# Linear attention before a mixture of experts: float32 projections in row halves, numerators in column halves, denominators in column quarters

## The chip, the cores and the metric

The kernel runs on one core of a Trainium2 chip. The metric is the device time of one execution in microseconds. Three timed runs of the kernel before gave a median of 1389.53 us (1389.01 to 1392.44).

## What is computed

Attention with feature maps, for 4 batches and 8 heads of 576 tokens with 64 features; then two layers of feed-forward networks on the 2304 tokens. The change is in the attention alone.

```python
def phi(x):
    proj = np.einsum('bhsd,df->bhsf', x, w_phi)                 # 64 -> 128 features
    proj = proj - np.max(np.abs(proj), axis=-1, keepdims=True)
    return np.concatenate([np.exp(proj), np.exp(-proj)], axis=-1)
q_p, k_p = phi(q), phi(k)
kv = np.einsum('bhsf,bhsd->bhfd', k_p, v)
z = np.sum(k_p, axis=2)
num = np.einsum('bhsf,bhfd->bhsd', q_p, kv)
den = np.einsum('bhsf,bhf->bhs', q_p, z)[..., None] + 1e-06
x = num / den       # then x = moe(x), and out = moe2(x)
```

## The kernel before

**Stages.** The attention stage treats 16 pairs of heads (4 batches by 4 pairs). The first 24 groups of products of the first MoE layer (12 up, 12 down, for the first 1536 tokens) are woven into it. The rest of that layer, and the second layer, come after it and are not edited. Up products for a block of 512 tokens need the attention outputs of every pair whose batch lies in that block, so the first block needs pairs 0 to 3.

**The order** of the attention stage is made ahead, in Python, by the class Plan. Each operation has a name, costs for the engines that may run it, the operations that it follows, a rank, and the buffers that it takes and reads. Plan.run takes again and again the operation that can begin first by these costs, ties by the lower rank (table RANK plus the pair's number). What it takes is emitted, and each engine then runs its instructions in that order.

**One pair of heads, by operations.**

- ld: DMAs on SP's queue bring k and q (128 rows: 64 features of each of two heads; 576 columns) and v. The ring kr, qr has one buffer each.
- two: k and q are split into a rounded high part (kh, qh, a cast on ScalarE or VectorE) and the rest (kl, ql, a subtraction on VectorE or GpSimd, L325).
- P (project, L339): for each of five token tiles (four of 128, one of 64) three float32r products over 256 columns, L348 to L350, against the block-diagonal weights wbh and wbl. Tiles go in units of two, two and one, each in one PSUM bank.
- R and S (largest L355, less L362): VectorE takes the largest magnitude of each row and subtracts it, into pmk and pmq.
- E: two exponentials of keys into ke (L368).
- KV (key_values, L379): v by ke, plain float32, one head in each column half of the array, so two products at a time. The sums over tokens (L387, ones by ke) go to the other half of the same PSUM bank, in column quarters. From pair 5 on (NZ) the four whole tiles are first added in pairs (Z, L392) and summed by add_up (L396).
- CV, TV, VH: key-values and sums are copied out (kvs), turned by TensorE (L409, and L411 for the sums) and copied into kvt, where each head's 128 columns hold 64 of key-values and 64 times the sums.
- T (turn_queries, L430) and X (L437): the queries are turned, ten transposes a pair, and the two exponentials taken into qe.
- A (attend, L447): per head and per half of the tokens (256 and 320) two plain float32 products with 128 weight columns, so that numerators and denominators come in one bank.
- D, N (take): denominators and numerators are copied out, four copies each, 64 rows high, into den and num (L144 is the copy helper).
- I (invert, L459 to L462): VectorE transposes the denominators in 32 by 32 blocks, adds 1e-6, takes the reciprocal, and transposes back.
- X0, X1, X2 (x_part): multiply, round, subtract, giving Xh and Xl for the MoE layer.

**Buffers.** PSUM has five banks in ring "bank" for P, T, TV and A, one bank "kv" for key-values and sums, and two banks "mm" for the woven MoE products (tile names mm; the same lines L231 and L252 serve the later ones as up and dn). Pair p may start its projections in the plan once the last A of pair p - 2 is placed (AHEAD = 2).

**Weights.** The first MoE layer's weights arrive as 64-bit words and are decoded in steps W, L554 to L565, by ScalarE, VectorE and GpSimd, in the same stage (tile acc_a).

Of the kernel before, what the change touches and what calls it, by code (L numbers as in the profile page):

```python
# [33 lines left out]
TILES = [(t * P, min(P, S - t * P)) for t in range(-(-S // P))]  # L34
UNITS = [(0, 1), (2, 3), (4,)]
HALVES = [(0, 256), (256, 320)]
HMAX = 320
# [14 lines left out]
    ld=6.41, sp=11.67, Pk=-7.81, Pq=-3.81, E=11.17, Z=-20.34, KV=-7.89, TV=-14.97, Q=-17.39, A=-0.59, F=2.88,  # L52
    W=22.69, U=16.42, G=5.73,
# [6 lines left out]
class Plan:  # L60
# [6 lines left out]
    WINDOW = 4096 / 1.2  # L67

    def __init__(self):
        self.ops, self.bufs, self.readers, self.begun = {}, {}, {}, set()  # L70

    def op(self, name, costs, after, rank, emit, alloc=(), reads=(), behind=(), late=0):
        self.ops[name] = (costs, after, rank, emit, alloc, {*after, *behind}, late)
        for x in reads:
            self.readers.setdefault(x, []).append(name)

    def run(self):
# [10 lines left out]
        def room(name):  # L88
            t = ready[name]
            for ring, key in self.ops[name][4]:  # L90
                if len(taken[ring]) >= self.bufs[ring]:
                    for x in self.readers[ring, taken[ring][-self.bufs[ring]]]:
                        t = max(t, done.get(x, np.inf))
            return t

        while ready:
            found = []
            for name in ready:
                t = room(name)
                if t < np.inf:  # L100
                    costs, rank = self.ops[name][0], self.ops[name][2]
                    begin = lambda e: max(t, free.get(e, self.START))
                    e = min(costs, key=lambda e: begin(e) + costs[e] + BIAS.get(e, 0))
                    found.append((begin(e), rank, order[name], name, e))
# [3 lines left out]
            cost = costs[e]  # L108
            if e == "t":
                k = int(start // self.WINDOW)  # L110
# [28 lines left out]
def fused(ctx: ExitStack, tc: tile.TileContext, qT, kT, v_main, v_tail, w_phi, alpha, probs, w64, wup, wdn, out):  # L139
# [19 lines left out]
    wbh = const.tile([P, 2, F], F32R, name="wbh")  # L159
    wbl = const.tile([P, 2, F], F32R, name="wbl")  # L160
# [4 lines left out]

    w0 = acc[0][:, 0, :2 * F].rearrange("p (h f) -> p h f", h=2)
# [110 lines left out]
    with ExitStack() as st1:  # L277
# [8 lines left out]
        for args in (  # L286
            ("kr", 1, F32, P, S), ("qr", 1, F32, P, S), ("v", 1, F32, P, len(TILES), 2, D),
            ("kh", 1, F32R, P, S), ("kl", 1, F32R, P, S), ("qh", 1, F32R, P, S), ("ql", 1, F32R, P, S),
            ("m", 13, F32, P, 4), ("pmk", 2, F32, P, 4, F), ("pmq", 3, F32, P, 4, F), ("ke", 2, F32, P, 4, 2, F),
            ("kvs", 1, F32, P, 4, F), ("qe", 4, F32, P, 2, HMAX), ("kvt", 4, F32, P, 4, P),  # L290
            ("den", 2, F32, P, S), ("dt", 1, F32, P, S), ("num", 2, F32, P, S), ("di", 3, F32, P, S // 32, 1),
            ("zsum", 1, F32, P, 4, 2 * F), ("gh", 4, F32R, P, BLK), ("gl", 4, F32R, P, BLK), ("t", 2, F32, P, BLK),
        ):
            ring(*args)
# [3 lines left out]
        ones = pool("ones", 1, st1).tile([P, 32], F32, name="ones")  # L298
# [21 lines left out]
        def two(name, key, src, srckey, n, after, prio, view=lambda x: x, shape=lambda x: x):  # L320

            op((name, "h", *key), hi_cost(n), after, prio, alloc=[(name + "h", key)],
               emit=lambda e: cp(engines[e], shape(new(name + "h", key)), view(tl[src, srckey])))
            op((name, "l", *key), lo_cost(n), [(name, "h", *key)], prio, alloc=[(name + "l", key)], reads=[(src, srckey)],
               emit=lambda e: engines[e].tensor_tensor(  # L325
                   shape(new(name + "l", key)), view(tl[src, srckey]), f32(shape(tl[name + "h", key])), ALU.subtract))

        pairs = [(b, j) for b in range(B) for j in range(NP)]

        def load(p, n):  # L330
            b, j = pairs[p]
            if n == "v":
                v = new("v", p)
                nc.sync.dma_start(v[:, :4], v_main[b, j])
                nc.sync.dma_start(v[:D, 4], v_tail[b, j])
            else:
                nc.sync.dma_start(new(n + "r", p), (qT if n == "q" else kT)[b, j])

        def project(p, n, u):  # L339
            xh, xl = tl[n + "h", (p,)], tl[n + "l", (p,)]  # L340
            unit = UNITS[u]
            rows = TILES[unit[0]][1]
            ps = new("bank", (n, p, u)).rearrange("p (m f) -> p m f", f=F)
            new("pm" + n, (p, u))
            for i, tile_ in enumerate(unit):
                o = ps[:rows, 2 * i:2 * i + 2, :]
                tok = slice(TILES[tile_][0], TILES[tile_][0] + rows)
# [4 lines left out]
        def largest(p, n, u):  # L352
            m, rows = 2 * len(UNITS[u]), TILES[UNITS[u][0]][1]
            ps = tl["bank", (n, p, u)].rearrange("p (m f) -> p m f", f=F)
            nc.vector.tensor_reduce(  # L355
                new("m", (n, p, u))[:rows, :m], ps[:rows, :m], AX.X, ALU.max, apply_absolute_value=True)

        def less(p, n, u):
            m, rows = 2 * len(UNITS[u]), TILES[UNITS[u][0]][1]
            ps = tl["bank", (n, p, u)].rearrange("p (m f) -> p m f", f=F)  # L360
            mx = tl["m", (n, p, u)][:rows, :m, None].to_broadcast([rows, m, F])
            nc.vector.tensor_tensor(tl["pm" + n, (p, u)][:rows, :m], ps[:rows, :m], mx, ALU.subtract)  # L362

        def exp_keys(p, u):
            m, rows = 2 * len(UNITS[u]), TILES[UNITS[u][0]][1]
            e = new("ke", (p, u))
            for s, sc in ((0, 1.0), (1, -1.0)):
                nc.scalar.activation(e[:rows, :m, s], tl["pmk", (p, u)][:rows, :m], AF.Exp, scale=sc)  # L368

        flat = lambda x: x.rearrange("p i s f -> p i (s f)")  # L370

        def key_values(p, u):

            unit = UNITS[u]
            rows, e, v = TILES[unit[0]][1], flat(tl["ke", (p, u)]), tl["v", p]
            kv = new("kv", p) if u == 0 else tl["kv", p]
            for i, tile_ in enumerate(unit):
                for h in range(2):
                    nc.tensor.matmul(  # L379
                        kv[h * D:(h + 1) * D, 0], v[:rows, tile_, h], e[:rows, 2 * i + h],  # L380
                        start=tile_ == 0, stop=tile_ == len(TILES) - 1, skip_group_check=True)
            if p >= NZ and u < 2:
                return
            for i, tile_ in enumerate(unit):
                for h in range(2):
                    r = 32 * (2 * (tile_ % 2) + h)
                    nc.tensor.matmul(  # L387
                        kv[r:r + 32, 1], ones[:rows], e[:rows, 2 * i + h],
                        start=False, stop=tile_ + 2 >= len(TILES), tile_position=(0, r), skip_group_check=True)

        def sum_keys(p, e):
            engines[e].tensor_tensor(new("zsum", p), flat(tl["ke", (p, 0)]), flat(tl["ke", (p, 1)]), ALU.add)  # L392

        def add_up(p):
            for m in range(4):
                nc.tensor.matmul(tl["kv", p][32 * m:32 * m + 32, 1], ones, tl["zsum", p][:, m],  # L396
                                 start=False, stop=True, tile_position=(0, 32 * m), skip_group_check=True)
# [15 lines left out]
        def copy_kv(p, k, e):  # L413
            b = tl["bank", ("kv", p)]
            o = tl["kvt", p].rearrange("p (h s) d -> p h s d", h=2)
            if k == 0:
                cp(engines[e], o[:, :, :, :D], b[:, :2 * P].rearrange("p (s h d) -> p h s d", s=2, h=2))
            else:
                z = b[:, 2 * P:3 * P].rearrange("p (s h d) -> p h s d", s=2, h=2)[:, :, :, 0:1]
                cp(engines[e], o[:, :, :, D:], z.to_broadcast([P, 2, 2, D]))  # L420

        def turn_queries(p, h, c):
            c0, n = HALVES[c]
            ps = new("bank", ("t", p, h, c))
            new("qe", (p, h, c))
            for u, unit in enumerate(UNITS):
                for i, tile_ in enumerate(unit):
                    t0, rows = TILES[tile_]
                    if c0 <= t0 < c0 + n:
                        nc.tensor.transpose(  # L430
# [532 lines left out]
```

## Time and profile before

| what | before |
|---|---|
| median of three runs | 1389.53 us |
| span of the profiled execution | 1389.4 us |
| TensorE busy | 1375.0 us, 99% |
| weight loads busy | 1166.5 us, 84% |
| VectorE busy | 779.9 us, 56% |
| ScalarE busy | 510.4 us, 37% |
| GpSimd busy | 283.1 us, 20% |

Busy times of TensorE include the time in which a product passes through the array while the next has begun, so a busy share of 99% is not a peak. The chain of waits is better to read: it follows back, from the last instruction, what released each step, and gives each piece the time by which it moved the chain on. A plain float32 product stands in the trace as two passes, each with a weight load (PEld); a float32r product and a transpose as one.

### The profile page before, as it was taken

Reading aid. Unit: us, or ns where it says so; the run is one execution under the profiler, and the core shown is the slowest. Engines: PE = TensorE matmul, PEld = TensorE weight load, DVE = VectorE, ACT = ScalarE, POOL = GpSimd, SP = SyncE. Lnnn points to the kernel's source line nnn. Section 1 sums busy time; section 2 is a strip of 40 time slices with the busy share of each in tenths; the row PEclk is TensorE's granted clock in tenths of the full one; section 3 lists DMA queues with packets and bytes.
Section 4 is the critical chain, followed back from the end, with each engine's and each line's share of the span. In section 5 each row is a group of like instructions: output and inputs, shape, how many; then the busy total and the mean of one; then the engine's idle time right before and its main releaser. Section 6 shows DMA issues by size and latency. Waiting matters only on the chain.

```text
span 1389.4 us, 19497 instructions
## 1 busy us (share of the span) xinstructions
PE 1375.0 (99%) x7216; PEld 1166.5 (84%) x7216; DVE 779.9 (56%) x1298; ACT 510.4 (37%) x1115; POOL 283.1 (20%) x278
## 2 busy tenths in 40 slices
PE   8999999999999999999999999999999999999998
PEld 5667767778888888889899889998999899989997
DVE  7995655679958855476445544633334363433342
ACT  6886666643213112125344443321222132211220
POOL 2344334222103004016556651000000000000000
PEclk9999999999999999999999999999999999999999
DMA  4322111022301103007977776665566667655541
GB/s 142 99 80 52 52 51 52 11 78 94 102 0 46 46 0 121 1 16 240 324 247 258 252 260 219 210 219 167 167 190 195 191 207 226 195 174 167 181 153 46
DMA packets 102207, 192.24 MB, mean 138 GB/s; under 512 B 11616, under 2 KB 12768, under 8 KB 102112
## 3 DMA queue, kind: packets, MB, share of 16 engines
q1 hardware_dynamic: 102112, 191.00, 42.7%
q8 instruction: 57, 0.93, 0.3%
q14 instruction: 38, 0.31, 0.1%
HBM read 140.10 MB, written 50.86 MB: 137 GB/s over the span
## 4 chain that ended last, share of the span: by engine, by line
PE 94%; DMA 2%; DVE 2%; ACT 1%; issue 0%; SPq 0%; POOL 0%; POOLq 0%; DVEq 0%; ACTq 0%
PE dn L871 28%; PE up L824 24%; PE up L231 12%; PE dn L252 12%; PE bank L447 4%; PE kv L379 3%; PE mm L252 2%; PE bank L348 2%; PE mm L231 2%; PE bank L430 2%; PE bank L349 1%; PE bank L350 1%; PE kv L387 1%; DMA w<-wdn 1%; PE kv L396 0%; DMA acc_a<-w 0%
## 5 line engine op out<-in xcount | busy, mean ns | idle before, releaser
L871 PE MATMUL dn<-whd,Xh 128*128 128x512 f32 x720 | 231.6, 391 | 0.0
L882 DVE SCALAR_TENSOR_TENSOR acc<-dn,pr,acc 128x512 f32<-128x512 f32 x126 | 88.7, 749 | 190.9 <-PE dn L871 190.9
L824 PE MATMUL up<-Xl,wlu 128*128 128x384 f32 x864 | 158.8, 335 | 1.3 <-DVE c L837 0.9
L871 PEld LDWEIGHTS dn<-whd,Xh 128*128 128x128 f32 x720 | 135.3, 188 | 26.9
L824 PEld LDWEIGHTS up<-Xl,wlu 128*128 128x128 f32 x864 | 150.3, 188 | 2.7 <-DVE c L837 1.8
L871 PE MATMUL dn<-Xh 128*128 128x512 f32 x648 | 151.8, 390 | 0.0
L837 DVE TENSOR_TENSOR c<-up,p 128x384 f32<-128x384 f32 x96 | 53.5, 557 | 175.1 <-PE up L824 175.1
L842 ACT COPY p<-up 128x384 f32<-128x384 f32 x48 | 23.0, 480 | 326.7 <-PE up L824 326.7
L871 PEld LDWEIGHTS dn<-Xh 128*128 128x128 f32 x648 | 121.7, 188 | 25.4
L871 PE MATMUL dn<-wld,Xh 128*128 128x512 f32 x360 | 141.0, 392 | 0.0
L824 PE MATMUL up<-Xl,whu 128*128 128x384 f32 x576 | 111.8, 335 | 0.8 <-ACT p L842 0.8
L831 ACT ACTIVATE Xh<-c 128x384 fp32r<-128x384 f32 x144 | 75.6, 526 | 79.7 <-DVE c L837 79.7
L824 PEld LDWEIGHTS up<-Xl,whu 128*128 128x128 f32 x576 | 101.2, 188 | 1.1 <-ACT p L842 1.1
L231 PE MATMUL up<-Xl,whu 128*128 128x512 f32 (+1 forms) x272 | 99.2, 365 | 0.0
L252 PE MATMUL dn<-gh,wld 128*128 128x512 f32 (+1 forms) x272 | 99.2, 365 | 0.0
L231 PE MATMUL up<-Xh,whu 128*128 128x512 f32 (+1 forms) x272 | 99.2, 365 | 0.0
L252 PE MATMUL dn<-gh,whd 128*128 128x512 f32 (+1 forms) x272 | 99.2, 365 | 0.0
L231 PE MATMUL up<-Xh,wlu 128*128 128x512 f32 (+1 forms) x272 | 99.2, 365 | 0.0
L252 PE MATMUL dn<-gl,whd 128*128 128x512 f32 (+1 forms) x272 | 99.2, 365 | 0.0
L176 ACT CAST gh<-t 128x512 fp32r<-128x512 f32 (+1 forms) x68 | 38.6, 569 | 149.3 <-DVE t L243 149.3
L832 DVE SCALAR_TENSOR_TENSOR Xh<-c,Xh 128x384 fp32r<-128x384 f32 x144 | 85.4, 594 | 5.5
L871 PEld LDWEIGHTS dn<-wld,Xh 128*128 128x128 f32 x360 | 67.6, 188 | 12.9
(171 smaller groups left out, 2498.7 us busy)
## 6 DMA issues: line engine op xcount, KB each, us to landing
whu<-wsu SPq DMA_DIRECT2D x96, 256.0 KB, 3.5
wlu<-wsu SPq DMA_DIRECT2D x96, 256.0 KB, 3.4
st<-w SPq DMA_DIRECT2D x24, 512.0 KB, 3.6
wsu<-whu SPq DMA_DIRECT2D x48, 256.0 KB, 3.3
wsu<-wlu SPq DMA_DIRECT2D x48, 256.0 KB, 3.2
Xh<-wsd SPq DMA_DIRECT2D x48, 256.0 KB, 3.8
wld<-wsd SPq DMA_DIRECT2D x40, 256.0 KB, 3.1
whd<-wsd SPq DMA_DIRECT2D x40, 256.0 KB, 3.4
```

Of the source, the lines that this page charges most:

```text
L176: nc.scalar.copy(hi, src)
L231: nc.tensor.matmul(ps[:, :bn], a[:, cs], x[:, cc, t0:t0 + bn], start=n == 0, stop=n == 3 * CC - 1)
L252: nc.tensor.matmul(ps, w[:, sl], g, start=start and k == 0, stop=stop and k == 2)
L348: nc.tensor.matmul(o, xh[:, tok], wbh, start=True, stop=False)
L379: nc.tensor.matmul(kv[h * D:(h + 1) * D, 0], v[:rows, tile_, h], e[:rows, 2 * i + h], start=tile_ == 0, stop=tile_ == len(TILES) - 1, skip ...
L447: nc.tensor.matmul(nd[:, :n], tl["kvt", p][:, 2 * h + s], tl["qe", (p, h, c)][:, s, :n], start=s == 0, stop=s == 1)
L824: nc.tensor.matmul(ps[name], w[k][:, r, kt * P:(kt + 1) * P], slots[k][:, x + kt], start=start and n == 0, stop=stop and n == 5, skip_grou ...
L831: nc.scalar.activation(gh, src, AF.Relu)
L832: nc.vector.scalar_tensor_tensor(gl, src, 0.0, f32(gh), ALU.max, ALU.subtract)
L837: nc.vector.tensor_tensor(o, ps[name], x, ALU.add)
L871: nc.tensor.matmul(ps[m], x[:, sl], w, start=c == chunks[0] and k == 0, stop=c == chunks[-1] and k == 2)
L882: nc.vector.scalar_tensor_tensor(av, ps[m], pe, av, ALU.mult, ALU.add)
```

## The change

- Projections are plain float32 products of the unsplit k and q with w_phi. Each head uses one half of the array's rows (64 features), the two heads write to two PSUM banks, and each bank takes four token tiles of 128 columns. The splits (two) and the tiles kh, kl, qh, ql, wbh, wbl go.
- The last 64 tokens of k and q of both heads go into one bank, with a head in each half of the columns (project_tails), so that a tile of tails has all 128 rows. R and S follow banks: four of 512 columns and one of 256 for a pair.
- Key-values: as before in column halves, in two parts instead of three; the tail's product takes all 128 rows against a v tile with zeros in the other head's rows (vts, two tiles zeroed once). The sums come after them in one operation (add_up), the tails with ones that are zero in the other head's rows.
- Queries are turned in nine transposes, not ten; the exponentials take 512 columns.
- Numerators: both heads at once, a head in each column half, 288 tokens a product. Denominators: an operation of their own, AD, in four groups of 32 columns (head by half of the tokens). VH becomes one copy.
- invert reads the denominators from PSUM; the reciprocals go, in eight instructions on 32 partitions and nine columns, to the rows in which the second transpose wants them. num is multiplied by the new tile rb.
- Z is two operations, one for each head. Rings: kr and qr have two buffers, pmq, ke, qe, kvt and others change, as the diff shows.
- Plan gets a mode for each TensorE operation (row, col, quarter, full, rounded), adds 100 ns to its cost at a change of mode and 0.57 to its rank there; RANK has other values (W from 22.69 to 40.35 among them).

Its core:

```diff
-            ("kr", 1, F32, P, S), ("qr", 1, F32, P, S), ("v", 1, F32, P, len(TILES), 2, D),
-            ("kh", 1, F32R, P, S), ("kl", 1, F32R, P, S), ("qh", 1, F32R, P, S), ("ql", 1, F32R, P, S),
-            ("m", 13, F32, P, 4), ("pmk", 2, F32, P, 4, F), ("pmq", 3, F32, P, 4, F), ("ke", 2, F32, P, 4, 2, F),
-            ("kvs", 1, F32, P, 4, F), ("qe", 4, F32, P, 2, HMAX), ("kvt", 4, F32, P, 4, P),
-            ("den", 2, F32, P, S), ("dt", 1, F32, P, S), ("num", 2, F32, P, S), ("di", 3, F32, P, S // 32, 1),
+            ("kr", 2, F32, P, S), ("qr", 2, F32, P, S), ("v", 1, F32, P, NM, 2, D),
+            ("m", 13, F32, P, 4), ("pmk", 2, F32, P, NM, F), ("pmq", 2, F32, P, NM, F), ("pmt", 2, F32, P, 2, F),
+            ("ke", 3, F32, P, NM, 2, F), ("ket", 2, F32, P, 2, F),
+            ("kvs", 1, F32, P, 4, F), ("qe", 2, F32, P, 2, 2, S), ("kvt", 2, F32, P, 3 * P),
+            ("dt", 1, F32, P, HS), ("di", 2, F32, P, HS // 32, 1), ("dj", 2, F32, P, S // 32, 1),
+            ("rb", 1, F32, P, S), ("num", 2, F32, P, S),
...
-                nc.tensor.matmul(o, xh[:, tok], wbh, start=True, stop=False)
-                nc.tensor.matmul(o, xh[:, tok], wbl, start=False, stop=False)
-                nc.tensor.matmul(o, xl[:, tok], wbh, start=False, stop=True)
...
+        def project(p, n):
+
+            x = tl[n + "r", p]
+            ps = [new("bank", (n, p, h)).rearrange("p (m f) -> p m f", f=F) for h in range(2)]
+            for i in range(NM):
+                for h in range(2):
+                    r = slice(h * D, (h + 1) * D)
+                    nc.tensor.matmul(ps[h][:, i], x[r, i * P:(i + 1) * P], w0[r, h], start=True, stop=True,
+                                     tile_position=(h * D, 0), skip_group_check=True)
+
+        def project_tails(p):
+            ps = new("bank", ("t", p))
+            for i, n in enumerate("kq"):
+                for h in range(2):
+                    nc.tensor.matmul(ps[h * TL:(h + 1) * TL, i * F:(i + 1) * F], tl[n + "r", p][:, NM * P:], w0[:, h],
+                                     start=True, stop=True, tile_position=(0, h * TL), skip_group_check=True)
...
+        def attend(p, c):
+
+            nd = new("bank", ("n", p, c))
...
             for s in range(2):
-                nc.tensor.matmul(nd[:, :n], tl["kvt", p][:, 2 * h + s], tl["qe", (p, h, c)][:, s, :n], start=s == 0, stop=s == 1)
...
+                for h in range(2):
+                    r = slice(h * D, (h + 1) * D)
+                    nc.tensor.matmul(nd[r, :HS], tl["kvt", p][:, s * P + h * D:s * P + (h + 1) * D],
+                                     tl["qe", p][:, h, s, c * HS:(c + 1) * HS], start=s == 0, stop=s == 1,
+                                     tile_position=(0, h * D), skip_group_check=True)
+
+        def denominators(p):
+            nd = new("bank", ("d", p))
+            for s in range(2):
+                for h in range(2):
+                    for c in range(2):
+                        r = 32 * (2 * h + c)
+                        nc.tensor.matmul(nd[r:r + 32, :HS], tl["kvt", p][:, 2 * P + s * D + h * 32:2 * P + s * D + (h + 1) * 32],
+                                         tl["qe", p][:, h, s, c * HS:(c + 1) * HS], start=s == 0, stop=s == 1,
+                                         tile_position=(0, r), skip_group_check=True)
...
-            nc.vector.transpose(dt, den)
+            nc.vector.transpose(dt, tl["bank", ("d", p)][:, :HS])
             nc.vector.tensor_scalar_add(di, dt.rearrange("p (k i) -> p k i", i=32)[:, :, 0:1], 1e-6)
-            nc.vector.reciprocal(di, di)
-            nc.vector.transpose(den.rearrange("p (k i) -> p k i", i=32), di.to_broadcast([P, S // 32, 32]))
+            for h in range(2):
+                for c in range(2):
+                    for to in range(2):
+                        a, o = (32 * (2 * h + x) for x in (c, to))
+                        nc.vector.reciprocal(dj[o:o + 32, c * n:(c + 1) * n], di[a:a + 32])
+            nc.vector.transpose(rb.rearrange("p (k i) -> p k i", i=32), dj.to_broadcast([P, S // 32, 32]))
```

## Rows read from the trace of the kernel before

**Rows 1.** Page, part 4: chain that ended last, whole span, by engine.

```profile
PE 94%; DMA 2%; DVE 2%; ACT 1%; issue 0%; SPq 0%; POOL 0%; POOLq 0%; DVEq 0%; ACTq 0%
```

**Rows 2.** Stretches: us; busy us of PE, PEld, DVE, ACT, POOL; clock, DMA.

```profile
35.00:80.00 45.00, 44.50 (x315) 30.03 (x313) 41.41 (x75) 39.66 (x96) 18.00 (x13) 1.00 0.37 104
154.10:275.90 121.80, 121.80 (x759) 85.94 (x758) 72.76 (x131) 81.06 (x201) 42.39 (x28) 1.00 0.15 40
```

**Rows 3.** Chain of waits from 154.1 to 275.9 us, shares by line.

```profile
by line: PE bank L447 24.9%; PE kv L379 15.0%; PE mm L252 11.4%; PE mm L231 9.0%; PE bank L348 8.6%; PE bank L430 7.9%; PE bank L350 6.7%; PE bank L349 6.6%; PE kv L396 3.3%; PE kv L387 3.2%; PE bank L411 2.3%; PE bank L409 1.3%
```

**Rows 4.** Groups of instructions, TensorE, 154.1 to 275.9 us: shapes, count, busy, mean ns.

```profile
L411 PE MATMUL bank<-sel,kvs 128*128 128x64 f32 x28 | 3.9, 262 | 0.0
```

**Rows 5.** Chain in order of time, 154 to 172 us: start, us, what.

```profile
159.76 1.01 PE kv L379 x8
160.78 0.26 PE bank L348
161.04 0.12 PE bank L349
...
162.79 1.73 PE bank L447 x8
164.51 0.44 PE bank L430 x4
164.95 0.58 PE kv L379 x4
165.53 0.55 PE kv L387 x4
166.08 1.27 PE bank L447 x4
167.36 0.57 PE kv L396 x8
...
169.99 0.39 PE bank L411 x4
```

**Rows 6.** Chain in order of time, 35 to 60 us: four products of sums.

```profile
44.98 0.57 PE kv L387 x8
```

**Rows 7.** Chain from 35 to 105 us, shares by line.

```profile
by line: PE bank L447 16.0%; PE kv L379 15.6%; PE bank L348 9.9%; PE mm L231 7.9%; PE bank L430 7.9%; PE kv L387 7.2%; PE bank L349 6.6%; PE bank L350 6.5%; DVE acc_a L558 3.1%; DVE m L355 2.3%; PE bank L411 2.2%; issue 2.1%; ACT ke L368 1.
```

**Rows 8.** Groups of instructions, VectorE, 154.1 to 275.9 us.

```profile
L355 DVE TENSOR_REDUCE m<-bank 128x4 f32<-128x512 f32 x28 | 17.9, 675 | 0.4 <-PE bank L350 0.3
L362 DVE TENSOR_TENSOR pmq<-bank,m 128x512 f32<-128x512 f32 x14 | 9.1, 676 | 0.0
...
L462 DVE STREAM_TRANSPOSE den<-di 128x576 f32<-128x576 f32 x7 | 5.5, 779 | 0.2
L355 DVE TENSOR_REDUCE m<-bank 64x2 f32<-64x256 f32 x14 | 5.4, 409 | 1.6 <-PE bank L350 1.4
...
L461 DVE RECIPROCAL di<-di 128x18 f32<-128x18 f32 x6 | 1.6, 267 | 0.2
...
L460 DVE TENSOR_SCALAR di<-dt 128x18 f32<-128x18 f32 x6 | 1.1, 179 | 0.2
```

**Rows 9.** Groups of instructions, ScalarE and GpSimd, 154.1 to 275.9 us.

```profile
L144 ACT COPY den<-bank 64x320 f32<-64x320 f32 x13 | 5.5, 421 | 4.6 <-PE bank L447 4.5
...
L144 ACT CAST qh<-qr 128x576 fp32r<-128x576 f32 x6 | 4.0, 675 | 11.6 <-POOL num L469 6.5 <-PE bank L349 5.1
...
L325 POOL TENSOR_TENSOR ql<-qr,qh 128x576 fp32r<-128x576 f32 x6 | 8.6, 1432 | 5.0 <-ACT qh L144 4.9
```

**Rows 10.** Timeline, 0 to 21 us: start, us, what, idle before.

```profile
3.65 0.67 ACT L144 CAST kh<-kr 128x576 fp32r<-128x576 f32 x1 [1.43 <-DMA kr<-kT]
...
4.22 0.40 ACT L176 CAST wbh<-acc_a 128x256 fp32r<-128x256 f32 x1
...
4.74 0.58 PE L348 MATMUL bank<-wbh,kh 128*128 128x256 f32 x1
...
7.45 0.68 DVE L355 TENSOR_REDUCE m<-bank 128x4 f32<-128x512 f32 x1
```

More of the change, by code (lines that the diff above doesn't have):

```diff
@@ L33 @@
 NB = len(BLOCKS)
[L34 to L37, printed above, removed]
+NM = S // P
+TL = S - NM * P
+HS = S // 2
 BLK2 = 384
@@ L89, in room, with turn @@
             t = ready[name]
+            more = {}
             for ring, key in self.ops[name][4]:
-                if len(taken[ring]) >= self.bufs[ring]:
-                    for x in self.readers[ring, taken[ring][-self.bufs[ring]]]:
+                n = more.get(ring, 0)
+                more[ring] = n + 1
+                if len(taken[ring]) + n >= self.bufs[ring]:
+                    for x in self.readers[ring, taken[ring][n - self.bufs[ring]]]:
                         t = max(t, done.get(x, np.inf))
             return t
+        mode = [None]
+        def turn(name, e):
+            return self.SWITCH if e == "t" and self.modes[name] != mode[0] else 0
         while ready:
@@ L107, in run @@
             costs, after, rank, emit, alloc, behind, late = self.ops[name]
-            cost = costs[e]
+            cost = costs[e] + turn(name, e)
             if e == "t":
+                mode[0] = self.modes[name]
                 k = int(start // self.WINDOW)
@@ new lines, in less, with exp_keys, exp_tails @@
+        def less(key):
+            m = segments(key)
+            ps = tl["bank", key][:, :m * F].rearrange("p (m f) -> p m f", f=F)
+            mx = tl["m", key][:, :m, None].to_broadcast([P, m, F])
+            nc.vector.tensor_tensor(new("pm" + key[0], key[1:]), ps, mx, ALU.subtract)
+        def exp_keys(p, h):
+            e = new("ke", (p, h))
+            for s, sc in ((0, 1.0), (1, -1.0)):
+                nc.scalar.activation(e[:, :, s], tl["pmk", (p, h)], AF.Exp, scale=sc)
+        def exp_tails(p):
+            e = new("ket", p)
+            for s, sc in ((0, 1.0), (1, -1.0)):
+                nc.scalar.activation(e[:, s], tl["pmt", (p,)][:, 0], AF.Exp, scale=sc)
@@ new lines, in add_up, with product @@
+        def add_up(p):
+            kv = tl["kv", p]
+            def product(par, h, a, e, stop):
+                r = 32 * (2 * par + h)
+                nc.tensor.matmul(kv[r:r + 32, 1], a, e, start=False, stop=stop, tile_position=(0, r), skip_group_check=True)
+            for i in range(1 if p >= NZ else 2):
+                for par in range(2):
+                    for h in range(2):
+                        e = tl["zsum", (p, h)][:, par] if p >= NZ else flat(tl["ke", (p, h)])[:, 2 * i + par]
+                        product(par, h, ones[:, 0], e, par == 1 and (i == 1 or p >= NZ))
+            for h in range(2):
+                product(0, h, ones[:, 1 + h], tail(tl["ket", p]), True)
@@ L399, in save_kv, with sum_keys @@
+        def sum_keys(p, h, e):
+            ke = flat(tl["ke", (p, h)])
+            engines[e].tensor_tensor(new("zsum", (p, h)), ke[:, :2], ke[:, 2:], ALU.add)
         def save_kv(p, k, e):
@@ L439, in attend, with copy_kv, turn_queries @@
-        def attend(p, h, c):
-            n = HALVES[c][1]
-            nd = new("bank", ("n", p, h, c))
-            if h == c == 0:
-                new("den", p)
+        def copy_kv(p, e):
+            cp(engines[e], new("kvt", p), tl["bank", ("kv", p)][:, :3 * P])
+        def turn_queries(p, h):
+            ps = new("bank", ("qt", p, h))
+            if h == 0:
+                new("qe", p)
+            if h == 2:
+                nc.tensor.transpose(ps[:, :P], tl["pmt", (p,)][:, 1], ident)
+                return
+            for i in range(NM):
+                nc.tensor.transpose(ps[:, i * P:(i + 1) * P], tl["pmq", (p, h)][:, i], ident)
@@ new lines, in fused @@
+            op(("PT", p), {"t": pe32(F, 2)}, [("ld", n, p) for n in "kq"], RANK["PT"] + p, alloc=[("bank", ("t", p))],
+               reads=[(n + "r", p) for n in "kq"], mode="col", emit=lambda e, p=p: project_tails(p))
+            for key in [(n, p, h) for n in "kq" for h in range(2)] + [("t", p)]:
+                pr_ = RANK["P" + key[0]] + p + 0.1 * (key[-1] if len(key) == 3 else 2)
+                cost = {"v": dve(segments(key) * F)}
+                op(("R", *key), cost, [("P", *key[:2]) if len(key) == 3 else ("PT", p)], pr_, alloc=[("m", key)],
+                   emit=lambda e, a=key: largest(a))
+                op(("S", *key), cost, [("R", *key)], pr_, alloc=[("pm" + key[0], key[1:])],
+                   reads=[("bank", key), ("m", key)], emit=lambda e, a=key: less(a))
@@ new lines, in fused @@
+            op(("ld", "v", p), {"d": 900}, [], RANK["ld"] + p, alloc=[("v", p), ("vt", p)], late=2000, emit=lambda e, p=p: load(p, "v"))
+            for h in range(2):
+                op(("E", p, h), {"a": 2 * act(NM * F)}, [("S", "k", p, h)], RANK["E"] + p + 0.1 * h, alloc=[("ke", (p, h))],
+                   reads=[("pmk", (p, h))], emit=lambda e, a=(p, h): exp_keys(*a))
+            op(("E", p, 2), {"a": 2 * act(F)}, [("S", "t", p)], RANK["E"] + p + 0.2, alloc=[("ket", p)],
+               reads=[("pmt", (p,))], emit=lambda e, p=p: exp_tails(p))
@@ new lines, in fused @@
+            xs = [("X", p, h) for h in range(3)]
+            for c in range(2):
+                pr_ = RANK["A"] + p + 0.1 * c
+                op(("A", p, c), {"t": pe32(HS, 2)}, [*xs[:2 + c], ("VH", p)], pr_, reads=[("qe", p), ("kvt", p)], behind=[("A", p, 0)] * c,
+                   alloc=[("bank", ("n", p, c))] + [("num", p)] * (c == 0), mode="col",
+                   emit=lambda e, a=(p, c): attend(*a))
+                op(("N", p, c), copy_cost(HS), [("A", p, c)], pr_,
+                   reads=[("bank", ("n", p, c))], emit=lambda e, a=(p, c): take(*a, e))
@@ L535, in fused @@
+            op(("X0", p), lo_cost(S), [("I", p)] + [("N", p, c) for c in range(2)], pr_, reads=[("rb", p)],
                emit=lambda e, p=p: x_part(p, 0, e))
@@ L602, in fused @@
                     g = (c, blk)
[L603 removed]
+                    op(("U", *g), {"t": pe(BLK, 12)}, have + [("W", 5, c, 0)], pr_, mode="rounded",
                        alloc=[("mm", g), ("gh", g)], emit=lambda e, a=g: up_products(*a, new("mm", a), new("gh", a)))
@@ L614, in fused @@
                     key = (cs, blk, i)
-                    op(("M", *key), {"t": pe(BLK, 3 * GRP)}, [("G2", c, blk) for c in cs] + [("W", 5, c, 1) for c in cs], pr_,
+                    op(("M", *key), {"t": pe(BLK, 3 * GRP)}, [("G2", c, blk) for c in cs] + [("W", 5, c, 1) for c in cs], pr_, mode="rounded",
                        alloc=[("mm", key)], reads=[(x, (c, blk)) for x in ("gh", "gl") for c in cs],
```

232 lines of the change are left out of this document (82 added, 150 removed).

## The prediction

> **What bounds the kernel now.** I first read the page's chain that ended last: 94% of the span is TensorE, with no other engine over 2% [rows 1]. That does not say whether the attention stage, the only one edited, is so bound. So I cut out a stretch of it, 154.1 to 275.9 us, which holds whole pairs of heads: the transposes of sums at L411 are four passes a pair, and 28 of them make seven pairs [rows 4]. The reader is to see three things. The granted clock there is 1.00, the upper level, 2.4 GHz, and VectorE is busy for 72.8 of 121.8 us, ScalarE for 81.1 [rows 2]. The chain through that stretch consists of TensorE lines alone [rows 3]. So a pass saved on TensorE there is time saved, and cheaper elementwise work is not, except where it keeps TensorE fed. Earlier, from 35 to 80 us, VectorE is busy for 41.4 of 45 and ScalarE for 39.7 [rows 2], and the chain of 35 to 105 us has some per cent of VectorE and "issue" pieces [rows 7]: there TensorE already waits a little.
>
> The chain gives the price of a pair. A pair takes 121.8 / 7 = 17.4 us; the MoE products woven in (lines L231 and L252 on tile mm) are 20.4% of it. The rest by share [rows 3]: numerators and denominators L447 24.9% = 4.33 us; projections L348 to L350 21.9% = 3.81; key-values L379 15.0% = 2.61; turned queries L430 7.9% = 1.37; sums L387 and L396 6.5% = 1.13; turned key-values L409 and L411 3.6% = 0.63. Together 13.88 us.
>
> **Prices of passes.** Eight passes of a plain float32 product over 256 columns take 1.73 us, 0.216 each, and a product is two passes [rows 5]. One pass of the float32r products takes 0.12, a transpose 0.44 / 4 = 0.11, and a pass whose moving side has only 64 columns but whose weights have 128 takes 0.39 / 4 = 0.098 [rows 5]. Column halves do run side by side: eight passes of key-values take 1.01 and four take 0.58 [rows 5], so four passes more cost 0.43, two at a time at 0.215, and 0.15 is left over at the start of the group. Column quarters run four at a time: eight passes of sums in 0.57 [rows 5], which is two rounds and 0.14. Coming out of such a group also costs: the first projection after one takes 0.26, not 0.12, and four 320-column passes take 1.27, not 4 x 0.27 [rows 5]; I take 0.17.
>
> As a test, the pair of before in these prices: projections 30 x 0.12 = 3.60, key-values 10 rounds 2.15, sums 4 rounds 0.86, transposes 10 x 0.11 = 1.10, turned key-values 0.63, L447 8 x 0.216 + 8 x 0.27 = 3.89; sum 12.23. The chain has 13.88, so 1.65 belongs to the five tile groups of a pair (three of key-values, two of sums): 0.71 for entering, about 0.65 for leaving, 0.29 not placed.
>
> **The change, part by part, on TensorE.** Projections: 30 rounded passes go. In their place are, for each of k and q, four tiles by two heads in row halves, 16 passes with the weights 128 columns wide. The trace has no two row halves at once. The bounds: side by side at 0.11 a round (eight rounds, 1.76 a pair), or one after another (3.52). I take 1.76, because column halves, the nearest row, gave the full factor. The tails of k and q come together in column halves: 8 passes of 128 columns, four rounds of 0.108 = 0.43.
>
> The Trainium skill, TensorE: Matmul & The Clock Gate, section Measured speedup vs the span model, has four row tiles gain 3.07, not 4; no run here shows it. By that share the eight rounds would be 2.29 and the result 8.5 us later.
>
> Key-values keep 10 rounds (2.15), the sums four (0.86). Transposes are 9, not 10, as both heads' tails now lie in one tile: 0.99. Turned key-values 0.63. Numerators: 8 products of 288 columns in column halves, 16 passes of 0.243 (0.27 x 288 / 320), 8 rounds = 1.94. Denominators: 16 passes in quarters, four rounds = 0.97. The two replace 3.89. Sum of rounds 9.73.
>
> Switching grows: nine tile groups now, not five (k, q, tails, two of key-values, sums, two of numerators, denominators). Where two of one mode follow each other the entry is saved; I count seven entries of 0.15, four and a half exits of 0.17 and keep the 0.29: 2.11. Bounds: 1.55 (five entries, three exits) and nine times 0.33 = 2.97. So a pair costs 9.73 + 2.11 = 11.84, which saves 2.04, and 16 pairs save 32.6 us (41.6 and 18.9 at the bounds).
>
> The first five pairs have two rounds of sums more. There a part of four products takes 0.57 [rows 6], and a pair has two such and one of 0.55: 1.69 against 6 x 0.215 + 0.15 = 1.44; beyond what the steady pair already counts that is 0.13 each, 0.6 in all.
>
> **Other engines.** Splits of k and q go: two casts of 0.67 and two GpSimd subtractions of 1.43 a pair [rows 9], nothing on the chain but at the start. There k lands by 3.65, its cast and that of w_phi come before the first product at 4.74, and VectorE's first reduction waits until 7.45 [rows 10]; unsplit, both can begin sooner. Bounds 0 to 4 us gained; I take 1, since the exponentials behind them still need two reductions and subtractions. Copies of denominators (0.42 each, four a pair [rows 9]) go too; numerators are copied in two whole-height halves. Reductions and subtractions of the tails become one of each, not two (0.41 [rows 8]): VectorE saves 0.8. The inversion grows: transposes of 0.78 [rows 8] become one of 288 columns from PSUM, 0.4 to 0.78, and one as before; one reciprocal of 0.267 over 18 columns becomes eight over 9 columns and 32 partitions, each between 0.13 (half of it) and 0.267 [rows 8]. I take 0.18, the row of the add over 18 columns: 1.44, so the inversion takes about 2.9, not 2.0. VectorE thus has about 10 us a pair as before, in a shorter pair. This lies beside TensorE's 11.8 plus woven MoE work. Where the cover is thin, before the MoE products begin, it may cost: 0 to 10 us; I take 1. Extra memsets on GpSimd, the third DMA of v and the deeper rings of k and q stand ahead of their use by several us and I cost them at nothing; SP's queue is in order, so a v load that must wait for its buffer holds the next k behind it, as before. The MoE products (0.23 a pass, 288 of them) are moved, not changed.
>
> **Sum.** The profiled execution's span is 1389.4, 0.1 from the median 1389.53, so nothing is added around it. 1389.4 - 32.6 - 0.6 - 1 + 1 = 1356. With the bounds 1344 to 1372.
>
> **Rivals.** (1) Row halves take turns, their weight loads above all: each load is 128 columns wide and takes as long as the 128 columns' two-cycle stream, so with no overlap each pass is paid alone: 1.76 more a pair, 28 us, 1384. Against it: L447's whole-array loads hide wholly behind the passes before (0.216 a pass) [rows 5], and column halves load together. For it: no row of row halves exists. The Trainium skill, TensorE: Matmul & The Clock Gate, section The mechanism, has weight loads overlap running products only where the row group differs. By that rule a half's second load would wait for its first pass, which gives the same 1384; L447's rows speak against it.
>
> (2) Slower: the five PSUM banks of ring "bank". Projections of one pair now claim two, two and one of them at once, where each claimed one before. A bank comes free only after VectorE's reduction and subtraction: four times 0.675 + 0.676 and once 0.41 + 0.41 [rows 8], 6.2 us. If all five are held together, transposes, turned key-values and numerators stand in TensorE's queue behind the banks; what needs none is key-values and sums, 3.3 us with their entries. That leaves about 3.2 us idle a pair, 51 us: 1407. It decides from 2.06 us a pair. Against it: MoE products use another ring and average 66 / 16 = 4.1 us a pair, and the chain of before, with as many banks, shows no such wait [rows 3]. For it: no MoE product can run before four pairs are done.
>
> (3) Better than my bounds: groups merge further and the shorter first chain lets pairs begin some us sooner, 1340.
>
> **How the numbers follow.** Forecast 0.74, (1) 0.12, (2) 0.09, (3) 0.05. The predicted time is the forecast's, 1356. To leave out no more than 2 in 10 the range runs from 1343 to 1384, which takes in the forecast's own range and half of (1). No measurement of this kernel tells 0.3%, 4.2 us, from no change, so faster means below 1385.3: 0.74 + 0.05 + 0.07 of (1) = 0.86; the same: 0.05 of (1) and 0.01 of (2) = 0.06; slower: 0.08 of (2).
>
> **What would show it.** Right: the four tiles of one projection last about 1.0 us on the chain, with pairs of records starting together; a numerator group of eight passes 1.1; the attention stage of whole pairs still all TensorE; first product of the MoE's next blocks some 33 us sooner. Wrong: a projection of 1.8 us and more (1); pieces of VectorE's m and pmk, or waits before L430's successor, in the chain (2); a clock below 1.00 in the stage; exits that cost 0.3.

## The result, and the profile after

The changed kernel takes 1353.37 us, the median of four runs (1352.19 to 1354.90), against 1390.40 for the kernel before in the same runs: a ratio of 0.9736, 95% interval 0.9722 to 0.9750, 37 us less. The span of the profiled execution is 1350.2 us (1389.4 before), 39.2 less; that execution took 1352.19, so 2.0 us of it lie outside the span.

The page of after, part 1 (TensorE) and part 4 (chain by engine); [rows 1] has the latter for before:

```profile
PE 1331.8 (99%) x7616; PEld 1130.8 (84%) x7616; DVE 776.5 (58%) x1365; ACT 443.3 (33%) x943; POOL 256.9 (19%) x268
...
PE 89%; DVE 7%; DMA 2%; ACT 1%; issue 1%; SPq 0%; POOL 0%; DVEq 0%; ACTq 0%; POOLq 0%
```

TensorE carries 89% of the chain, not 94%, and VectorE 7%, not 2%. Where, is seen by stretches, as in [rows 2] (us; busy us of PE, PEld, DVE, ACT, POOL; clock, DMA share, GB/s). The second holds six whole pairs:

```profile
35.00:105.00 70.00, 63.27 (x611) 42.49 (x611) 65.24 (x133) 40.58 (x97) 24.65 (x18) 0.95 0.30 88
118.50:201.65 83.15, 83.15 (x787) 57.16 (x788) 60.53 (x139) 47.02 (x112) 27.29 (x20) 1.00 0.23 65
```

In 35 to 105 us VectorE is busy for 65.2 of 70 us and TensorE for 63.3. The same stretch before:

```profile
35.00:105.00 70.00, 68.96 (x468) 47.90 (x466) 64.29 (x113) 58.73 (x139) 30.46 (x23) 1.00 0.31 88
```

VectorE was about as busy then (64.3 us); it is TensorE that now stands idle, for 6.7 us and not 1.0, and its granted clock is 0.95, not 1.00. From 118 us on TensorE is busy throughout. The chain there, shares by line, and then one pair in order of time (start, us, what), answer to [rows 3] and [rows 5]:

```profile
by line: PE bank L349 15.8%; PE kv L392 15.6%; PE bank L458 15.1%; PE mm L260 14.4%; PE bank L468 8.0%; PE bank L440 7.4%; PE mm L239 7.1%; PE kv L401 6.1%; PE bank L356 4.2%; PE bank L427 2.8%; PE bank L425 2.7%; PE bank L437 0.8%
```

```profile
131.24 1.09 PE bank L349 x16
132.33 0.37 PE bank L425 x2
132.70 0.39 PE bank L427 x4
133.09 1.09 PE bank L349 x16
134.19 2.99 PE mm L260 x12
137.18 1.12 PE bank L458 x8
138.30 1.02 PE bank L440 x8
139.32 0.11 PE bank L437
139.43 0.59 PE bank L356 x8
140.02 0.86 PE kv L392 x8
140.88 0.97 PE bank L458 x8
141.85 1.29 PE kv L392 x12
143.15 1.11 PE bank L468 x16
144.26 0.85 PE kv L401 x12
```

These 14 pieces are the whole pair: 13.87 us, of which 2.99 are a group of twelve MoE products (L260), so 10.88 us for the pair; before it was 13.88. That group follows a projection here, and its change of mode stands in its own piece: six groups in the second stretch average 2.98, where the nine of before, in 154.1 to 275.9 us, average 2.76. The reader is to see three things. A projection of 16 passes takes 1.09. Numerators (L458) take 1.12 and 0.97, denominators (L468) 1.11. And several groups pay no entry at all. Eight passes of key-values take 0.86, four rounds of 0.215 and nothing more; the tails before them (L356) and the numerators behind them use the same column halves. The numerators behind those key-values take 0.97, the others, behind the full-array MoE products, 1.12. Sums of twelve passes take 0.85 right behind the denominators, both in quarters.

The first stretch is the other half of the story. The chain of after from 0 to 105 us, shares by line, and a part of it in order of time:

```profile
by line: DVE m L365 13.2%; DVE dj L485 9.4%; issue 6.6%; DVE pmq L371 5.7%; DVE pmk L371 5.3%; PE kv L392 4.7%; DVE acc_a L199 4.6%; DVE acc_a L197 4.5%; DVE rb L486 4.4%; DVE acc_a L201 3.7%; DMA kr<-kT 3.5%; PE bank L468 3.2%; PE kv L401 
```

```profile
27.34 0.49 DVE dt L479
...
27.86 0.18 DVE di L480
...
28.07 0.20 DVE dj L485
...
29.84 0.78 DVE rb L486
30.62 1.17 DVE m L365 x2
31.79 1.20 DVE pmk L371 x2
32.99 1.20 DVE m L365 x2
34.18 1.20 DVE pmq L371 x2
35.38 0.40 DVE dt L479
```

For these 8 us the chain does not touch TensorE: VectorE inverts one pair's denominators (dt, di, eight pieces of dj, rb), then reduces and subtracts the next pair's projections (m, pmk, m, pmq), then begins the next inversion.

TensorE's clock takes a small part too. TensorE waited for 2.12 us, until 93.59 us, for a pmq; in 95 to 100 us the granted clock is 0.66, the lower level of 1.2 GHz for part of the time, and two groups stand in the chain with 1.71 and 1.59 us where a whole pair has 0.86 and 0.97:

```profile
95.67 1.71 PE kv L392 x8
97.38 1.59 PE bank L458 x8
```

### The profile page after: what moved, and what is told of

The parts are those of the page before. It is cut to its first block, busy times and chain, and to the rows that moved or that the text cites. A ratio compares the mean times of both kernels' runs of the same rounds, so it can differ in the third digit from the quotient of the medians.

```text
span 1350.2 us, 20101 instructions
## 1 busy us (share of the span) xinstructions
PE 1331.8 (99%) x7616; PEld 1130.8 (84%) x7616; DVE 776.5 (58%) x1365; ACT 443.3 (33%) x943; POOL 256.9 (19%) x268
## 4 chain that ended last, share of the span: by engine, by line
PE 89%; DVE 7%; DMA 2%; ACT 1%; issue 1%; SPq 0%; POOL 0%; DVEq 0%; ACTq 0%; POOLq 0%
PE dn L901 29%; PE up L854 25%; PE up L239 12%; PE dn L260 12%; PE mm L260 2%; PE kv L392 2%; PE bank L458 1%; PE bank L349 1%; DVE m L365 1%; PE bank L468 1%; DVE dj L485 1%; PE mm L239 1%; PE kv L401 1%; PE bank L440 1%; DVE pmk L371 1%
## 5 line engine op out<-in xcount | busy, mean ns | idle before, releaser
L260 PE MATMUL dn<-gh,wld 128*128 128x512 f32 (+1 forms) x272 | 99.1, 364 | 0.0
L260 PE MATMUL dn<-gh,whd 128*128 128x512 f32 (+1 forms) x272 | 99.1, 364 | 0.0
L260 PE MATMUL dn<-gl,whd 128*128 128x512 f32 (+1 forms) x272 | 99.0, 364 | 0.0
```

The source lines that it names most:

```text
L260: nc.tensor.matmul(ps, w[:, sl], g, start=start and k == 0, stop=stop and k == 2)
```

## The experiments

Each ratio is to the kernel before, run beside it; the changed kernel stands at 1353.4 us and 0.9736.

**Row halves one after the other.** In project:

```diff
-            for i in range(NM):
-                for h in range(2):
+            for h in range(2):
+                for i in range(NM):
```

> The changed kernel with the loops of project turned round: all four tiles of one head, then all four of the other, so that no two passes of different row halves stand next to each other until the heads change. The work is the same. Theory (row halves run side by side in the changed kernel): a projection's 16 passes go from 1.09 us on the chain to about 1.09 + 8 x 0.11 = 1.97 us; 20 projections lie in the stretch that TensorE bounds (from about 105 us), 12 in the one that VectorE bounds, so between 17.6 and 28 us more, 1371 to 1381. Rival (halves take turns in the changed kernel already, the saving comes from elsewhere): no change, 1353 within 3.

1366.5 us, ratio 0.9817 (0.9791 to 0.9844), 13 more, below the theory's 1371. The chain of this kernel, one projection:

```profile
153.66 1.64 PE bank L349 x16
```

1.64 and not 1.09, nor the 1.97 of two halves wholly in turn: the records show the second head's first pass 0.55 us after the first head's, which leaves some overlap. From the 8th pair's turned key-values (L427, 125.62 us) to the 13th's (200.41) a pair takes 14.96 us, 1.09 more than in the changed kernel, which is two projections at 0.55. So the halves do run side by side in the changed kernel, weight loads of 128 columns included, and that is worth at least 1.1 us a pair where TensorE sets the pace. The 13 us are not a clean price: in the profiled execution the first pair's L427 begins 6.0 us later than in the changed kernel (23.69 against 17.73), with a granted clock of 0.85 and not 1.00 in the first 35 us, and one of the four runs took only 1361.75.

**Column groups in another order.** In attend and denominators the loop over s goes inside those over heads and column groups:

```diff
-            for s in range(2):
-                for h in range(2):
+            for h in range(2):
+                for s in range(2):
...
-            for s in range(2):
-                for h in range(2):
-                    for c in range(2):
+            for h in range(2):
+                for c in range(2):
+                    for s in range(2):
```

> The changed kernel with the loops of the numerators and of the denominators turned round, so that both passes of a column group come before the next group's: same work, neighbours in the same columns. Theory (halves and quarters run side by side): numerators go from 2.09 to about 4.0 us a pair and denominators from 1.11 to about 4.0, 4.8 us a pair; in the ten pairs that TensorE bounds 48 us, in all sixteen 77: 1400 to 1430. Rival (the passes overlap whatever their order, since the queue looks ahead): no change, 1353 within 3.

1355.0 us, ratio 0.9742 (0.9718 to 0.9766): no difference that these intervals can show. The theory's expectation missed; the chain of this kernel:

```profile
157.98 1.02 PE bank L458 x8
...
160.29 1.13 PE bank L468 x16
```

Numerators 1.02 (0.97 in the changed kernel), denominators 1.13 (1.11). Passes of other columns start although passes of the same columns stand ahead of them in the program. So this run does not price the packing; the next comes nearer to it.

**Numerators and denominators as before, the rest as changed.** attend, take, copy_kv and the one reciprocal of the kernel before, their operations in full mode; for room kr and qr have one buffer.

```diff
-                for h in range(2):
-                    r = slice(h * D, (h + 1) * D)
-                    nc.tensor.matmul(nd[r, :HS], tl["kvt", p][:, s * P + h * D:s * P + (h + 1) * D],
...
+                nc.tensor.matmul(nd[:, :n], tl["kvt", p][:, 2 * h + s], tl["qe", p][:, h, s, c0:c0 + n], start=s == 0, stop=s == 1)
```

> The changed kernel with the numerators and denominators of the kernel before: products with 128 weight columns on the whole array, eight copies out, one reciprocal; projections, key-values and queries as changed. For room k and q have one buffer each. Theory (each part of the change is worth its TensorE time): numerators and denominators go from 3.2 us a pair to 3.9 and 0.2 for a later exit, about 1 us in each of ten bound pairs, and in the early six VectorE gains the 1 us that TensorE loses: 1360 to 1366. Rival (the packed numerators gain nothing, their reciprocals eat it): 1350 to 1356.

1374.0 us, ratio 0.9888 (0.9873 to 0.9903), 20.6 more. That is above what I expected, and far from the rival: this part carries more than half of the 37 us. From 105 to 250 us its chain is TensorE alone, a quarter of it the products L464:

```profile
by line: PE bank L464 25.7%; PE mm L261 16.0%; PE kv L392 14.5%; PE mm L240 13.9%; PE bank L349 11.1%; PE kv L401 6.2%; PE bank L446 5.3%; PE bank L356 3.2%; PE bank L427 2.2%; PE bank L425 1.3%; PE bank L443 0.8%; issue 0.0%
```

That is 37.3 of 145 us for the 132 passes recorded there, 4.5 for the sixteen of a pair, where the changed kernel's numerators and denominators take 3.20; 1.3 more in each of sixteen pairs would be 21. The order and two buffer counts differ too, so 20.6 is the part's worth in this program and not a clean price.

**The planner without modes.**

```diff
-    SWITCH = 100
-    STAY = 0.57
+    SWITCH = 0
+    STAY = 0
```

> The changed kernel whose planner knows nothing of modes: the added cost of a change (100 ns) and the added rank (0.57) are zero, everything else as it is. Theory (a steady pair takes 10.9 us and not the 11.84 of the forecast because the order puts tile groups of one kind together): groups fall apart, 0.5 to 1 us a pair, 8 to 16 us more, 1361 to 1369. Rival (ranks alone make that order): no change, 1353 within 3.

1352.7 us, ratio 0.9725 (0.9704 to 0.9746): the same; the theory's 8 to 16 us did not come. The order of TensorE differs in many places, and it is no worse. In its chain, too, groups of one kind meet (from 149.87 us: tails 0.59, key-values 0.86, numerators 0.97). So what the planner adds for a change of mode is not needed for that; the ranks alone bring it.

**Less for VectorE in the first stretch.** Three of the four steps of decoding the first eight weight tiles are left out, first in the changed kernel, then in the kernel before:

```diff
             elif 2 <= k < 3:
+                if k != 2.5:
+                    return
                 word(int(4 * (k - 2)), w, u, lo, hi)
```

> The changed kernel without three of the four VectorE steps of decoding the first eight weight tiles (the steps L195, L197 and L201: those weights are then wrong); 20 us less work for VectorE, nearly all before 105 us. The order of all else is as it was. Theory (VectorE sets the pace of the first 105 us of the changed kernel): 8 to 19 us less, 1335 to 1345. Rival (TensorE sets the pace throughout, as the forecast had it): 0 to 3 us less, 1350 to 1353.

1343.1 us, ratio 0.9664 (0.9648 to 0.9680), 10.3 less than the changed kernel. Not all of it need be VectorE's time as such: the granted clock in 35 to 105 us is 1.00 here and 0.95 in the changed kernel, by estimate up to 3.5 us (0.05 of 70).

> The kernel before without the same three steps (those weights are then wrong), 18 us less work for VectorE before 117 us. Theory (there TensorE sets the pace, with 14.5 us a pair): 0 to 6 us less, 1384 to 1390. Rival (VectorE, busy for 41.4 of 45 us there, set the pace before too): 10 to 18 us less, 1372 to 1380.

1387.7 us, ratio 0.9990 (0.9981 to 1.0000): 1 to 3 us. The same work hides in the kernel before and does not in the changed one. Without it in both, the change is worth 44.6 us and not 37.

**One reciprocal and eight copies on ScalarE.**

```diff
+            nc.vector.reciprocal(di, di)
...
-                        nc.vector.reciprocal(dj[o:o + 32, c * n:(c + 1) * n], di[a:a + 32])
+                        nc.scalar.copy(dj[o:o + 32, c * n:(c + 1) * n], di[a:a + 32])
```

> The changed kernel with one reciprocal over 128 partitions and 9 columns, and eight copies on ScalarE that put it where the second transpose wants it, as an operation of their own in the plan. Theory (VectorE sets the pace of the first 105 us, where eight reciprocals take 1.7 us a pair): 1.4 us less for VectorE in each of the first six pairs, so 4 to 9 us less, 1344 to 1349. Rival (the length of the chain through the inversion sets the pace there, not VectorE's load): eight copies of about 0.19 us make it no shorter, 0 to 5 us more, 1353 to 1358.

1349.0 us, ratio 0.9699 (0.9678 to 0.9719), 4.4 less than the changed kernel: within the theory's range, at its near end, and the fastest version here that computes the whole reference. The split of the inversion into three operations changed the order as well.

**Each reciprocal twice.**

```diff
-                        nc.vector.reciprocal(dj[o:o + 32, c * n:(c + 1) * n], di[a:a + 32])
+                        for _ in range(2):
+                            nc.vector.reciprocal(dj[o:o + 32, c * n:(c + 1) * n], di[a:a + 32])
```

> The changed kernel with each of the eight reciprocals issued twice: 1.7 us more for VectorE in each pair, TensorE's work and all orders unchanged. Theory (VectorE sets the pace in the first six pairs and TensorE after them): about 6 x 1.7 = 10 us more, 1360 to 1366, and nothing in the later pairs. Rival A (TensorE sets the pace throughout): 0 to 2. Rival B (VectorE throughout): 16 x 1.7 = 27, 1380.

1385.6 us, ratio 0.9978 (0.9968 to 0.9988), 32 more: nearly the whole gain is gone, and my theory with it. The later pairs, which I held for TensorE's, grew from 13.86 us to 16.07 on average (table below). Four of those five take 15.74, the fifth 17.42, with a granted clock of 0.66 in 205 to 210 us. The chain of this kernel in one of them, in order of time:

```profile
151.20 0.78 DVE rb L487
151.98 1.18 DVE m L365 x2
153.16 1.20 DVE pmk L371 x2
154.35 1.20 DVE m L365 x2
155.55 0.61 DVE pmq L371
...
156.20 1.26 PE bank L440 x8
...
161.28 1.15 PE bank L468 x16
...
162.46 0.49 DVE dt L479
```

It is a loop over two in-order queues. VectorE's inversion stands ahead of the next pair's reductions (m, pmk, m, pmq); TensorE's transposes of queries (L440) need the first pmq and stand ahead of the products that lead to the next denominators (L468), for which the next inversion waits. TensorE's timeline shows it waiting, once a pair:

```profile
156.20 1.26 PE L440 MATMUL bank<-ident,pmq 128*128 128x128 f32 x8 [1.64 <-DVE pmq L371]
```

The changed kernel's timelines show VectorE's two subtractions for pmq, of which the first ends at 151.83, and then TensorE's transposes, which follow without a wait:

```profile
151.16 1.27 DVE L371 TENSOR_TENSOR pmq<-bank,m 128x512 f32<-128x512 f32 x2
```

```profile
152.10 1.09 PE L440 MATMUL bank<-ident,pmq 128*128 128x128 f32 x8
```

So the loop had some 0.3 us to spare. What came is 1.9: here the second transpose (rb) begins 3.76 us after the first reciprocal (163.18 to 166.94), in the changed kernel 1.84 (158.92 to 160.76). And after a wait the eight transposes take 1.26 on the chain, not 1.02. 1.9 less 0.3, and 0.24, is about the 1.88 by which four of the pairs grew.

**The same work for VectorE outside the loop.** Formed after that run: eight reciprocals of constants ahead of the first transpose of the inversion.

```diff
+            for _ in range(2):
+                for o in range(0, P, 32):
+                    nc.vector.reciprocal(dj[o:o + 32, :n], ones[o:o + 32, 0, :n])
             nc.vector.transpose(dt, tl["bank", ("d", p)][:, :HS])
```

> The changed kernel with eight reciprocals more a pair, as many as in the run that doubled them (1.7 us of VectorE), but of constants and ahead of the transpose of the denominators, where VectorE stands waiting for them for 3.4 us in a steady pair. TensorE's work and all orders are unchanged. Theory (in a steady pair it is the loop denominators, inversion, next pair's reductions, its transposes, next denominators that must not grow; VectorE's load alone is hidden): nothing in the later pairs, and in the first six, where VectorE is busy 93 to 97%, 0 to 10 us: 1353 to 1364. Rival (VectorE's load sets the pace throughout): 30 us as in that run, 1380 to 1388.

1364.9 us, ratio 0.9820 (0.9804 to 0.9837), 11.5 more, just above the theory's range and 21 below the other placing. When the turned key-values of each pair begin (timeline, line L427) tells where it is lost:

| kernel | 8th pair, us | 13th pair, us | a pair between |
|---|---|---|---|
| changed | 118.70 | 188.02 | 13.86 |
| reciprocals twice | 133.06 | 213.42 | 16.07 |
| as many ahead of the transpose | 129.49 | 198.80 | 13.86 |
| decoding left out | 110.96 | 180.26 | 13.86 |

The later pairs are untouched; nearly all the loss, 10.8 us, lies before the eighth pair (where the granted clock is lower as well: 0.90 in 35 to 70 us). VectorE's timeline in a later pair (start, us, what, idle before) shows the added work inside its wait:

```profile
123.83 1.86 DVE L481 RECIPROCAL dj<-ones 32x9 f32<-32x9 f32 x8
127.41 0.48 DVE L482 STREAM_TRANSPOSE dt<-bank 128x288 f32<-128x288 f32 x1 [1.73 <-PE bank L468]
```

## Why the prediction was right, and where its steps were not

The time (1356 against 1353.4), the range and the sign held. But the sum is one of spans: the prediction added nothing around the span, while 2.0 us lie outside it here, and 1.8 in a run of the kernel before (1388.68 against 1386.9). Span against span it is 1356 against 1350.2. Two of its sums do not come out either: all bounds at once give 1343 to 1380, not 1344 to 1372, and 6.2 less 3.3 us in rival (2) is 2.9, which gives 1402. The range would have been the same. By its steps:

- **TensorE sets the pace of the stretch of whole pairs.** Right, before and after: both chains are TensorE lines alone. But it has only about 0.3 us a pair to spare against the loop through VectorE, which the forecast did not see; doubling the reciprocals showed that, and the same work outside the loop showed that it is the loop and not VectorE's load.
- **Row halves run side by side.** Right: 1.09 a projection where I had 0.88 and a share of the switching; with the halves' order turned it is 1.64. Rival (1) fell. So did its time of 1384 by the Trainium skill, TensorE: Matmul & The Clock Gate, section The mechanism, as I had applied it to a half's second load: its rule lets a load overlap products of another row group, and with the halves alternating the loads cost nothing that these rows show.
- **Sum of rounds 9.73.** Right where the pieces have no entry beside them: key-values 0.86 and 1.29 are the 2.15, the second numerators 0.97 of 1.94, the sums 0.85 of 0.86. Numerators were to be 1.94 and denominators 0.97 a pair without entries; they are 2.09 and 1.11 with them.
- **Switching 2.11.** Too much, outside my bounds (1.55 to 2.97). Measured: 10.88 - 9.73 = 1.15 a pair. I had counted entries by group; in the order that was made, tails, key-values and numerators follow each other in one kind, and sums follow denominators in another. So the pair's own pieces saved 3.00 and not 2.04: 48 us over sixteen, not 32.6. One exit the forecast left out, as it took the MoE products for moved and not changed: the 0.22 by which their group is longer behind a tile group. Twelve groups stand so, up to 230 us, which takes back 2.6; 45.4 are left.
- **VectorE's cover in the first stretch, 1 us taken of 0 to 10.** Too little: of 45.4 + 0.6 the span shows 39.2, so 6.8 us are missing, and leaving out decoding, which gave 1 to 3 us before, gives 10.3 in the changed kernel. Its inputs were near: eight reciprocals at 0.205 against my 0.18, the transpose from PSUM 0.48 against 0.4 to 0.78. What I missed is that a shorter TensorE pair turns VectorE, at 92% before, into the bound there, and that TensorE's granted clock falls once TensorE has to wait (0.95 against 1.00 in 35 to 105 us).
- **The start, 1 us gained.** None at its first step: the first projection begins at 4.74 us as before [rows 10]. It waited for the eight warm-up passes that TensorE runs from 1.19, not for casts. VectorE's first reduction came 0.8 sooner. The timeline of after:

```profile
1.19 3.62 PE L657 MATMUL mm<-acc_a 128*32 128x256 f32 x8 [1.19 <-DVE acc_a L654]
...
4.74 1.91 PE L349 MATMUL bank<-w,kr 64*128 64x128 f32 x16
...
6.68 1.29 DVE L365 TENSOR_REDUCE m<-bank 128x4 f32<-128x512 f32 x2 [5.55 <-PE bank L349]
```

- **Rival (2), the banks.** Not seen, though two of the signs listed are there in the first stretch, m and pmk in the chain and a clock below 1.00. Up to 118 us TensorE's waits end with pmq of VectorE (4.6 us) and kvs of ScalarE (4.2); the projections, which claim the banks, waited for the DMA of k (1.6) and never for VectorE.

So two terms of the sum were mis-sized: TensorE's saving by 12.8 us to one side, VectorE's cover by 5.8 to the other, with 1 more for the start. They cancel in part and leave the span 6 under the forecast, and the time outside the span hides part of that. In whole pairs the forecast's mechanism is shown; that its number came so near is partly luck.

## What to carry to other kernels

Price a tile mode by its rounds, and its switches by what stands next to it in the order, not by the count of groups. When the engine that sets the pace gets shorter, look for the stretch in which the next one has no room left, and for the loop through both in-order queues: eight more reciprocals a pair cost 32 us inside that loop and 11.5 outside it, what TensorE's clock lost by its waits included. Before a second engine takes on eight small instructions a pair, see whether a third can place one result eight times.

## What the runs showed of the hardware

Passes of different column groups overlap even if the program has them group by group: denominators 1.13 against 1.11 us. Row halves with eight passes each in a row overlapped only in part, 1.64 against 1.09 us. The column groups had four passes each in a row, so the length of the rows differs as well as their kind; which of them decides was not tried.

A VectorE step with all its data in SBUF can wait for a GpSimd one. The decoding step L195 takes 0.42 us alone, and here 1.60 and 1.63. VectorE's timeline and then GpSimd's, of the changed kernel:

```profile
38.86 1.60 DVE L195 TENSOR_SCALAR acc_a<-acc_a 128x512 uint32<-128x512 uint32 x1
...
41.31 1.63 DVE L195 TENSOR_SCALAR acc_a<-acc_a 128x512 uint32<-128x512 uint32 x1
```

```profile
38.77 1.41 POOL L493 TENSOR_TENSOR num<-num,rb 128x576 f32<-128x576 f32 x1 [3.13 <-DVE rb L486]
40.96 1.70 POOL L497 TENSOR_TENSOR Xl<-num,Xh 128x576 fp32r<-128x576 f32 x1 [0.78 <-ACT Xh L155]
```

Both long steps start during a GpSimd step and end about 0.3 us after it. The Trainium skill, SBUF — State Buffer, section SBUF: two separate sides, says that GpSimd and certain VectorE steps (in a two-port mode, or with two inputs in SBUF) share a pair of ports, which one of them holds for a whole instruction while the other is blocked. These rows agree in the waiting; whether L195 runs in a two-port mode no row shows. Ten such waits before 100 us, about 10 us together, fall in the stretch that VectorE bounds; how much of the time they cost was not tried.
